# Where the activations between two matrix products begin in on-chip memory: eight starting places instead of one

## The chip, the cores and the metric

The kernel runs on one core of a Trainium2 chip. TensorE (PE) multiplies matrices: it loads a 128x128 block of weights (the stationary operand, a row "PEld LDWEIGHTS" in the trace) and then streams a second operand past it (the moving operand, "PE MATMUL"), and adds the result up in PSUM. VectorE (DVE) and ScalarE (ACT) work element by element, GpSimd (POOL) does little here, and SyncE (SP) issues most transfers from the main memory into SBUF, the on-chip memory from which both operands of a product are read. SBUF has 128 partitions; an address here is a byte offset inside a partition, the same in all 128.

The metric is the device time of one execution, in microseconds (us).

## The reference

Causal attention (2 batches, 12 heads, 448 positions, head size 64) is followed by two MLPs on the 896 rows of 768 values that it leaves. All is float32.

```python
scores = scale * np.matmul(q, k.transpose(0, 1, 3, 2))
scores = np.where(mask, -1000000000.0, scores)
attn = softmax(scores)                      # written out in the reference
x = np.matmul(attn, v) -> (896, 768)
h = np.maximum(x @ w_in, 0.0);   x = h * h @ w_out         # first MLP, 768 -> 2048 -> 768
h = x @ w_in2;  g = h - np.tanh(h);  out = g @ w_out2      # second MLP
```

## The kernel before, in words

**Attention.** For 12 pairs of heads the kernel makes scores, the exponentials, transposes of the probabilities and the product with the values. The scores, exponentials and transposes of neighbouring pairs are interleaved. The result is x, with features on the partitions: six tiles x0 to x5, each with a high and a low part (rounded value and remainder) for both batches.

**The MLPs.** Each MLP is cut in two halves of 1024 hidden features. For each half come 16 groups of the first product (8 blocks of 128 hidden features, two batches; function `first`) and then 12 groups of the second product (6 blocks of 128 output features, two batches; function `second`). A group adds up in one PSUM bank, over the blocks k of the contraction (6 in a first product, 8 in a second one), three matmuls each: high weights by high activations (line 428), high weights by low activations (line 429), low weights by high activations (line 430). Each loads 128 weights columns and streams 448 columns (one batch). So there are 4 x 16 x 6 x 3 = 1152 matmuls in the first products (PSUM tile h, moving operand x in the first MLP and y in the second) and 4 x 12 x 8 x 3 = 1152 in the second products (PSUM tile o, moving operand g).

**Between the products.** The hidden activations go through ACT and DVE (`act1`: relu and square; `act2`: the value less its tanh) and are written as a high part (line 438, ACT) and a low part (line 441, DVE) into tiles called g. One tile g holds two feature blocks of one batch, high and low: 4 x 448 words of 4 bytes. There are eight of them, in eight slots of SBUF that the attention used for its probabilities and values. Function `gdst` makes the tile when the first of its two blocks comes.

**Weights.** A weight arrives as a float64 in pieces of 128 x 768 (tile raw). DVE and ACT turn each piece into high and low float32 parts (tile w, a ring of eight). This work is woven into the rest by a budget of costs; it depends on the order of the calls alone, not on addresses.

**Addresses.** Each slot of a g tile has 64 words (256 bytes, `LINE`) more than the tile needs, so that the data can begin anywhere in the first 256 bytes. The table `G_AT` says where, by slot. Four slots begin at 192 above a multiple of 256 bytes, and four at 96; with 56 or 16 words added, every g tile begins at 160 above a multiple of 256. Inside a tile all parts lie at multiples of 256 bytes from its beginning. The tiles x and y, which SBUF's allocation puts there without a table, also begin at 160 above a multiple of 256, and all weight blocks begin at 96. So modulo 256 each moving operand of the MLPs begins 64 bytes above the weight block that it meets.

The order of all instructions and the waits between them follow from the order of the calls in the program; the change reaches the kernel through `gdst`, called by `early` (which does six groups of the first product during attention) and by `first`.

Of the kernel before, what the change touches and what calls it, by code (L numbers as in the profile page):

```python
# [27 lines left out]
NPAIR = B * NP  # L28
NQ = S // D
RING = 8  # L30
LINE = 64
G_AT = (56, 56, 56, 16, 16, 16, 16, 56)
UNIT = 6
# [52 lines left out]
def body(ctx: ExitStack, tc: tile.TileContext, qT, kT, vL, w1, w2, w3, w4, out):  # L86
# [9 lines left out]
    def slot(i, shape, dt, name):  # L96
        return sb.tile(shape, dt, tag=f"slot{i}", name=name)
# [72 lines left out]
    def ring(u):  # L170
        taken.append(u)
        return sb.tile([P, 2, UC], F32R, tag="w", bufs=RING, name=f"w{u}")

    def room():
        i = len(taken) - RING
        return i < 0 or taken[i] < freed[0]
# [317 lines left out]
    gt = {}  # L494

    def gdst(l, half, m, b):

        if m % 2 == 0:
            i = (5, 6, 0, 1, 3, 2, 4, 7)[4 * b + m // 2]
            n = 2 * 2 * S  # L500
            t = slot(i, [P, n + LINE], F32R, f"g{l}_{half}_{b}_{m // 2}")
            gt[b, m // 2] = t[:, G_AT[i] : G_AT[i] + n].rearrange("p (z k s) -> p z k s", z=2, k=2)
        t = gt[b, m // 2]
        g[m, b] = (t[:, 0, m % 2], t[:, 1, m % 2])
        return g[m, b]
# [5 lines left out]
    def first(l, half, m, b):  # L511

        u = (2 * l + half) * 2 * HALF + m
        dst = gdst(l, half, m, b)
        h = hbank(f"h{u}_{b}")
        for _ in first_pieces(l, half, m, b, h):
            pass
        if b == 1:
            freed[0] = u + 1
        return lambda: (act1, act2)[l](h, dst)  # L520


    def early(count):
        for m in range(count):
            dst = gdst(0, 0, m, 0)
            h = ps.tile([P, 512], F32, tag="h", bufs=1, name=f"h{m}_0")[:, :S]
            for k, _ in enumerate(first_pieces(0, 0, m, 0, h)):
                if k == KD - 1:
                    done.append((h, dst))
                yield  # L530
# [61 lines left out]
    for s in range(NPAIR + 2):  # L592
        p, a = s - 1, s - 2
# [162 lines left out]
```

## Time and profile before

| what | value |
|---|---|
| median of 3 runs | 541.25 us (541.24 to 541.47) |
| the profiled execution | 540.64 us |
| its span, first to last instruction | 538.9 us |
| busy PE, PEld, DVE, ACT | 532.3, 482.3, 345.9, 327.4 us |

The profiled execution has 1.7 us outside its span. "Busy" of PE counts from a matmul's start to its modelled end, and neighbouring matmuls overlap, so the distance between starts says more than the busy share: it is what the next matmul costs. The MLPs without the six early groups take the span from about 96 us to its end; attention comes before.

### The profile page before, as it was taken

The numbers are of one execution on the slowest core, as the hardware profiler recorded it, in microseconds if no ns is written. First come the engines' busy times: TensorE is split into PE (matmuls) and PEld (weight loads), VectorE is DVE, ScalarE is ACT, GpSimd is POOL, SyncE is SP. The second block draws the span as 40 slices with busy tenths as digits, with TensorE's granted clock in tenths as the row PEclk, the third lists the DMA queues.
The fourth block names the chain that finished last, engine by engine and source line by source line (L and its number), as shares of the span: only waits on it lengthen the run. The fifth ranks groups of instructions, "written<-read, shape, count | busy, mean of one in ns | idle before, by whom it ended". The sixth has DMA issues, their size and how long they took to land.

```text
span 538.9 us, 8256 instructions
## 1 busy us (share of the span) xinstructions
PE 532.3 (99%) x3206; PEld 482.3 (90%) x3206; DVE 345.9 (64%) x730; ACT 327.4 (61%) x630; POOL 3.0 (1%) x21
## 2 busy tenths in 40 slices
PE   8999999999999999999999999999999999999997
PEld 5677878899999999999999999999999999999996
DVE  6998996664525155544554688988653588887301
ACT  6999996677424276664342388876643687854100
POOL 1000000000000000000000000000000000000000
PEclk9999999999999999999999999999999999999999
DMA  8851332352534233331333230113655301026111
GB/s 312 296 191 56 115 92 98 108 185 108 182 114 140 94 121 114 117 118 58 118 111 123 65 112 0 60 58 117 234 177 177 117 1 58 1 68 220 50 52 51
DMA packets 16022, 61.86 MB, mean 115 GB/s; under 512 B 1712, under 2 KB 7344, under 8 KB 15984
## 3 DMA queue, kind: packets, MB, share of 16 engines
q1 hardware_dynamic: 15696, 61.00, 33.6%
q8 instruction: 25, 0.41, 0.3%
q10 hardware_dynamic: 288, 0.34, 0.2%
q14 instruction: 13, 0.11, 0.1%
HBM read 58.59 MB, written 2.75 MB: 114 GB/s over the span
## 4 chain that ended last, share of the span: by engine, by line
PE 92%; DVE 6%; DMA 1%; ACT 0%; issue 0%; DVEq 0%; POOLq 0%; ACTq 0%
PE h L428 15%; PE o L429 14%; PE h L429 14%; PE o L428 14%; PE h L430 14%; PE o L430 14%; PE o L380 3%; DVE p L315 3%; PE t L368 2%; DVE p L354 2%; PE s L300 2%; DMA k<-kT 1%; DVE x L416 0%; ACT pt L375 0%; DVE w L155 0%; DVE raw L139 0%
## 5 line engine op out<-in xcount | busy, mean ns | idle before, releaser
L429 PE MATMUL o<-g,w 128*128 128x448 f32 x384 | 139.4, 363 | 0.0
L428 PE MATMUL o<-g,w 128*128 128x448 f32 x384 | 139.2, 362 | 0.0
L430 PE MATMUL o<-g,w 128*128 128x448 f32 x384 | 138.2, 360 | 0.0
L428 PEld LDWEIGHTS o<-g,w 128*128 128x128 f32 x384 | 72.1, 188 | 5.7
L430 PEld LDWEIGHTS o<-g,w 128*128 128x128 f32 x384 | 71.8, 187 | 5.0
L429 PEld LDWEIGHTS o<-g,w 128*128 128x128 f32 x384 | 72.1, 188 | 3.7
L428 PE MATMUL h<-x,w 128*128 128x448 f32 x192 | 71.4, 372 | 0.0
L429 PE MATMUL h<-x,w 128*128 128x448 f32 x192 | 69.7, 363 | 0.0
L429 PE MATMUL h<-y,w 128*128 128x448 f32 x192 | 69.7, 363 | 0.0
L428 PE MATMUL h<-y,w 128*128 128x448 f32 x192 | 69.6, 362 | 0.0
L430 PE MATMUL h<-x,w 128*128 128x448 f32 x192 | 69.3, 361 | 0.0
L430 PE MATMUL h<-y,w 128*128 128x448 f32 x192 | 69.1, 360 | 0.0
L139 DVE SCALAR_TENSOR_TENSOR raw<-raw 128x768 int32<-128x768 int32 x64 | 61.0, 954 | 11.7 <-ACT raw L125 11.7
L142 ACT CAST w<-raw 128x768 fp32r<-128x768 f32 x56 | 50.3, 898 | 26.7 <-DVE raw L139 26.7
L125 ACT ACTIVATE raw<-raw 128x768 f32<-128x768 f32 x64 | 58.7, 917 | 0.0
L155 DVE TENSOR_TENSOR w<-raw,w 128x768 fp32r<-128x768 f32 x32 | 30.6, 957 | 34.3 <-ACT w L142 34.1
L441 DVE TENSOR_TENSOR g<-r,g 128x448 fp32r<-128x448 f32 x32 | 20.0, 624 | 41.1 <-ACT g L438 41.1
L570 ACT COPY part<-o 128x448 f32<-128x448 f32 x24 | 12.8, 533 | 55.1 <-PE o L430 55.1
L153 DVE SCALAR_TENSOR_TENSOR w<-w,raw 128x768 fp32r<-128x768 f32 x32 | 30.6, 956 | 23.0 <-ACT w L142 22.9
L333 ACT ACTIVATE p<-p,st 128x320 f32<-128x320 f32 (+6 forms) x84 | 41.0, 512 | 3.3 <-DVE st L315 3.2
L428 PEld LDWEIGHTS h<-x,w 128*128 128x128 f32 x192 | 36.1, 188 | 3.1
L428 PEld LDWEIGHTS h<-y,w 128*128 128x128 f32 x192 | 36.0, 188 | 2.9
(57 smaller groups left out, 722.8 us busy)
## 6 DMA issues: line engine op xcount, KB each, us to landing
raw<-w SPq DMA_DIRECT2D x64, 768.0 KB, 4.2
q<-qT SPq DMA_DIRECT2D x12, 224.0 KB, 4.9
k<-kT SPq DMA_DIRECT2D x11, 224.0 KB, 3.8
out<-part SPq DMA_DIRECT2D x11, 224.0 KB, 1.9
v<-vL SPq DMA_DIRECT2D x2, 576.0 KB, 7.0
v<-vL SPq DMA_DIRECT2D x1, 1152.0 KB, 6.0
k<-kT ACTq DMA_DIRECT2D x1, 224.0 KB, 3.6
vend<-vL SPq DMA_DIRECT2D x2, 96.0 KB, 6.9
```

Source lines behind the costliest of these rows:

```text
L125: nc.scalar.activation(h, h, AF.Prelu, scale=2.0**-112, alpha=2.0**32)
L139: nc.vector.scalar_tensor_tensor(out=lo, in0=hi, scalar=3, in1=lo, op0=ALU.logical_shift_left, op1=ALU.bitwise_or)
L142: act_late.append(lambda: nc.scalar.copy(out=st["w"][:, 0], in_=lo.bitcast(F32)))
L153: nc.vector.scalar_tensor_tensor(out=w[:, 1], in0=w[:, 0].bitcast(F32), scalar=-(1.0 - 2.0**-24), in1=f, op0=ALU.mult, op1=ALU.add)
L155: nc.vector.tensor_sub(out=w[:, 1], in0=f, in1=w[:, 0])
L315: nc.vector.tensor_tensor_reduce(out=prob[n % 3][:, POFF[c] : POFF[c] + w], in0=sc.pop((n, c)), in1=mask[:, BEFORE - D * DIAG[c] :][:, :w] ...
L333: nc.scalar.activation(p, p, AF.Exp, bias=st[:, 0, i : i + 1], scale=-1.0, **kw)
L380: return nc.tensor.matmul(ob[n][D * j : D * j + D, o], lhsT=vs[b][kc][rows, D * h : D * h + D], rhs=rhs, skip_group_check=True, **flags).ins
L428: nc.tensor.matmul(h, lhsT=hi, rhs=xh, start=(k == 0), stop=False)
L429: nc.tensor.matmul(h, lhsT=hi, rhs=xl, start=False, stop=False)
L430: nc.tensor.matmul(h, lhsT=lo, rhs=xh, start=False, stop=(k == kk - 1))
L441: nc.vector.tensor_sub(out=dst[1], in0=v, in1=dst[0])
```

## The change

A second table, by layer, half and batch, is added to the place of the first one, modulo 64 words. Nothing else is changed: the tiles' sizes, slots, order and waits are the same, and the instruction streams of all engines are the same row by row apart from line numbers.

```diff
 RING = 8
+G_ADD = (56, 60, 62, 4, 12, 24, 28, 36)
 LINE = 64
 G_AT = (56, 56, 56, 16, 16, 16, 16, 56)
...
             t = slot(i, [P, n + LINE], F32R, f"g{l}_{half}_{b}_{m // 2}")
-            gt[b, m // 2] = t[:, G_AT[i] : G_AT[i] + n].rearrange("p (z k s) -> p z k s", z=2, k=2)
+            at = (G_AT[i] + G_ADD[4 * l + 2 * half + b]) % LINE
+            gt[b, m // 2] = t[:, at : at + n].rearrange("p (z k s) -> p z k s", z=2, k=2)
```

In bytes, modulo 256, the g tiles then begin as follows; the last column is the distance from the weight blocks (at 96), which is 64 in all eight cases before. Each row stands for 144 matmuls.

| layer, half, batch | g begins at | above the weights by |
|---|---|---|
| first MLP, half 0, batch 0 | 128 | 32 |
| first MLP, half 0, batch 1 | 144 | 48 |
| first MLP, half 1, batch 0 | 152 | 56 |
| first MLP, half 1, batch 1 | 176 | 80 |
| second MLP, half 0, batch 0 | 208 | 112 |
| second MLP, half 0, batch 1 | 0 | 160 |
| second MLP, half 1, batch 0 | 16 | 176 |
| second MLP, half 1, batch 1 | 48 | 208 |

The tiles x and y, and with them all first products, stay at a distance of 64.

## Rows read from the trace of the kernel before

**Rows 1.** Page: the span, and parts 1 and 2 (PE and granted clock)

```profile
span 538.9 us, 8256 instructions
...
PE 532.3 (99%) x3206; PEld 482.3 (90%) x3206; DVE 345.9 (64%) x730; ACT 327.4 (61%) x630; POOL 3.0 (1%) x21
...
PE   8999999999999999999999999999999999999997
...
PEclk9999999999999999999999999999999999999999
```

**Rows 2.** Page, part 4: the chain that ended last, by engine

```profile
PE 92%; DVE 6%; DMA 1%; ACT 0%; issue 0%; DVEq 0%; POOLq 0%; ACTq 0%
```

**Rows 3.** Stretches: length, busy us (count) of PE, PEld, DVE, ACT; second: tile g

```profile
109.68:533.88 424.20, 424.20 (x2123) 397.60 (x2122) 251.60 (x380) 233.56 (x373) 0.00 (x0) 1.00 0.31 104
...
96.00:540.00 444.00, 231.05 (x1152) 215.95 (x1152) 36.66 (x59) 32.48 (x58) 1.00 0.31 103
```

**Rows 4.** Order of time: start us, us, engine, line; first products, then second, then the end

```profile
109.67 0.36 PE L428 MATMUL h<-x,w 128*128 128x448 f32 x1
...
110.27 0.36 PE L428 MATMUL h<-x,w 128*128 128x448 f32 x1
...
299.87 0.36 PE L428 MATMUL o<-g,w 128*128 128x448 f32 x1
299.87 0.19 PEld L429 LDWEIGHTS o<-g,w 128*128 128x128 f32 x1
...
300.07 0.36 PE L429 MATMUL o<-g,w 128*128 128x448 f32 x1
...
300.47 0.36 PE L428 MATMUL o<-g,w 128*128 128x448 f32 x1
...
533.87 0.36 PE L428 MATMUL o<-g,w 128*128 128x448 f32 x1
```

**Rows 5.** Groups by form: count, busy us, mean ns of one, idle us before

```profile
L428 PEld LDWEIGHTS o<-g,w 128*128 128x128 f32 x384 | 72.1, 188 | 5.7
...
L430 PEld LDWEIGHTS o<-g,w 128*128 128x128 f32 x384 | 71.8, 187 | 5.0
...
L429 PEld LDWEIGHTS h<-y,w 128*128 128x128 f32 x192 | 36.0, 188 | 1.8
...
L368 PEld LDWEIGHTS t<-ident,p 128*128 128x128 f32 x168 | 19.0, 141 | 4.6 <-issue 1.3 <-DVE p L354 1.0 <-ACT pt L375 0.5
```

**Rows 6.** Groups that write g and wait, 98 to 536 us, same columns; then two waits

```profile
L441 DVE TENSOR_TENSOR g<-w,g 128x448 fp32r<-128x448 f32 x32 | 19.8, 618 | 4.5 <-ACT g L438 4.5
...
L438 ACT CAST g<-w 128x448 fp32r<-128x448 f32 x32 | 17.7, 554 | 3.1 <-DVE w L480 3.1
...
L441 DVE TENSOR_TENSOR g<-r,g 128x448 fp32r<-128x448 f32 x27 | 16.9, 625 | 40.7 <-ACT g L438 40.7
...
L438 ACT CAST g<-r 128x448 fp32r<-128x448 f32 x26 | 14.8, 568 | 0.8
...
ACT part L570 <- PE o L430: 55.1, 22, 4.3
...
ACT r L445 <- PE h L430: 23.1, 24, 3.0
```

## The prediction, on record before the changed kernel ran

> **What bounds the kernel now.** I read the page first. PE is busy 532.3 of 538.9 us, and the granted clock is full in all 40 slices [rows 1], which is the 2.4 GHz level. The chain that ended last is 92% PE [rows 2]. So, after attention, the time is the number of matmuls by the distance between their starts, and nothing else counts unless it makes PE wait.
>
> The windows give that distance. From 109.68 to 533.88 us PE is busy for all of the 424.20 us, with 2123 matmuls [rows 3]. Two of them began before the window, so 2121 starts share 424.20 us: 200.0 ns each. The order of time shows it at both ends: L428 starts at 109.67 and 110.27 in a first product, at 299.87 and 300.47 in a second one, and the stretch ends with a start at 533.87, so three matmuls take 0.60 us, and 707 such steps of 0.60 us are exactly the 424.20 us [rows 4]. There is not one gap, and x, y and g cost the same, whatever slot the g tile is in and whatever weight block it meets. Addresses that differ by multiples of 256 bytes therefore make no difference here; what no row of this kernel varies is the distance modulo 256, which is 64 everywhere.
>
> The groups show what the 200.0 ns hold. At 2.4 GHz and one column a tick, 448 columns need 186.7 ns; the rest is an excess of 13.3 ns. The next weight load starts together with a matmul (299.87 and 299.87 [rows 4]) and takes 187 to 188 ns, in second and first products alike, while a load of the same 128 columns takes 141 ns beside the short matmuls of the transposes [rows 5]. So beside a stream of 448 columns a load is 188 - 141 = 47 ns longer, and it ends some 12 ns before the next matmul starts. I read it thus: PE's two reads, of weights and of moving data, hold each other up, and the load ends late enough that it may be what spaces the matmuls. The trace can't prove the second half of that.
>
> **The change part by part.** It adds, removes and reorders no instruction, wait or transfer. It has three edits in effect.
>
> First, writes. ACT writes the high part and DVE the low part of g in new places. From 98 us on these are 26 + 32 writes of 568 and 554 ns on ACT, and 27 + 32 of 625 and 618 ns on DVE [rows 6], 69.2 us together. I price the edit at nothing: in the long stretch ACT is busy 233.56 and DVE 251.60 of 424.20 us [rows 3], and ACT waits 55.1 us for PE before L570 and 23.1 us before L445 [rows 6]. Were each write 10% longer, 6.9 us more would go into 363 us of idle time. Only the last writes ahead of a second product have little time; 10% of a pair of 554 and 618 ns is 0.12 us, so with four products that bounds the loss at 0.5 us. A gain there can't reach PE, since PE waits for nothing.
>
> Second, the first products. x and y stay where they are: 1152 matmuls, no change.
>
> Third, the second products: 1152 matmuls with the moving operand g, together 231.05 us of PE's busy time [rows 3]. Their distance from the weights goes from 64 bytes to 32, 48, 56, 80, 112, 160, 176 and 208, 144 matmuls each. Each ns by which the mean distance between starts changes is 1152 x 1 ns = 1.15 us. No row shows another distance, so I bound it. Below: the whole excess goes, 13.3 x 1152 = 15.4 us less; a stream can't be shorter than its columns. Above there is no such floor: the excess may double, 15.4 us more, and if the load took its 47 ns once more and every matmul waited for it, 54.1 us more. That last end is far from any row, since all 707 steps show the reads mostly hidden; I keep the doubling as the upper bound that counts.
>
> Which value? The slack on the two sides is unequal. A load that ends earlier can give back no more than 13.3 ns; a load that ends later pushes the next matmul at once, with 12 ns between them. Where two streams meet is set by their phase, so I expect places near the old one (32, 48, 56 and 80, all within 32 bytes of 64, the first MLP) to cost about what it costs, and those far from it (112, 160, 176 and 208, the second MLP) to lie between no change and a doubling. I take half the excess for these, 6.7 ns, midway because no row is nearer to either end: 144 x 4 x 6.7 ns = 3.85 us, and nothing for the near four. The profiled execution, 540.64 us, becomes 544.5; the median of the runs lies 0.6 us above that execution, so 545.1 us.
>
> The Trainium skill speaks against a change: its page "TensorE: Matmul & The Clock Gate", section "Step-by-step: what each phase is for", says that weights and moving data come through two independent read ports, so that loading the next weights takes no bandwidth from the running matmul; the page "SBUF — State Buffer", section "Who interferes with whom", adds that PE waits for no one. By that rule the time would be 541.25 us. The 188 ns load beside 141 ns [rows 5] does not fit it without more; it is the rule behind the first rival.
>
> **The rivals.** No effect of the address. Then all second products keep 200.0 ns, and the time is 541.25 us, within 0.2% (1.1 us, about what a measurement of this kernel can tell from no change). For it: no engine's work disturbs the 0.60 us steps, x, y and g agree to the row, and the 141 ns of the transposes may owe to their shorter stream, so that the 188 ns is merely how a load beside a long stream is recorded. Against: the excess of 13.3 ns is there, and the one quantity that could move it is never varied. The same time comes out if near and far places balance. 0.17.
>
> Faster: 64 bytes is a bad distance, and the loads meet the stream most there. Moving off it lets a load end sooner, until the stream bounds alone. If half the places lose the whole excess, 576 x 13.3 ns = 7.7 us go: 533.6 us; if a quarter of it goes everywhere, 3.8 us: 537.4 us. It decides from a mean of 199.1 ns on. For it: the excess exists, so there is something to win. Against: three matmuls take 600 ns in every step, with nothing that looks like a worst case, and the floor is close. 0.16.
>
> Slower by more: the near four suffer as the far four do, or the excess doubles in most places. All eight at a full doubling give 541.25 + 15.4 = 556.6 us; beyond that the load would bound openly. It is the upper part of my own case: 0.19 of its 0.67 above 550 us. A mechanism for it is the start of the stream: if the first reads of weights and data fall on the same piece of memory, the load falls behind at once and does not catch up.
>
> That the change does not do what it says: the starting places follow from the slots' addresses, and none of the eight is 64 above the weights, so this has no chance of its own. A second bound can't take PE's place: DVE has 172.6 us idle in the stretch [rows 3].
>
> **How the numbers follow.** Slower by places far from 64: 0.67, with 545.1 us and its own range of 542.4 to 556.6. No effect: 0.17, 541.25. Faster: 0.16, 537.4 for most of it, 526 at the floor. I count 0.66 slower, 0.18 same and 0.16 faster, since a little of the first case is too small to see. The range goes from 539.0 (the faster case's smaller half inside) to 556.6 (the doubling): some 0.10 is left out below and 0.08 above.
>
> **What would show it.** The order of time gives each second product by itself. Right: first products still at 0.60 us for three matmuls; in the second MLP's second products three matmuls take about 0.62 us (200.0 + 6.7 ns each), in the first MLP's 0.60 us; the granted clock stays 1.00; weight loads of the slower groups take longer than 188 ns; the steps alternate between the two batches of one half, since these have different places. Wrong in size: all eight moved, or only one place (152, the only one that is no multiple of 16). Wrong in kind: 0.60 us everywhere, or less than 0.60 us in any second product; or unchanged steps and a PE that idles before second products, which would mean the writes of g.

## The result, and the profile after

The changed kernel takes 545.09 us (median of 3 runs, 544.98 to 545.39) against 541.25 us: the ratio is 1.0071, with a 95% interval of 1.0048 to 1.0094. It is slower by 3.84 us, as forecast in sign and size (545.1 us). The parts of the forecast were less good than their sum, as the rows and runs below show.

The profiled execution has a span of 543.2 us, 4.3 us more than before. The page of the kernel after answers to [rows 1, 2]:

```profile
span 543.2 us, 8256 instructions
...
PE 536.4 (99%) x3206; PEld 482.7 (89%) x3206; DVE 346.2 (64%) x730; ACT 327.7 (60%) x630; POOL 3.0 (1%) x21
...
PEclk9999999999999999999999999999999999999999
...
PE 92%; DVE 6%; DMA 1%; issue 0%; ACT 0%; DVEq 0%; POOLq 0%; ACTq 0%
```

PE's busy time grew by 4.1 us; DVE and ACT have what they had, and the clock is full. Next, the long stretch [rows 3] cut at the borders of the products: from the first second product to the last, in turn second (g), first (x or y), second and so on. The columns are the stretch, its length, and busy us with counts for PE, PEld, DVE, ACT and POOL, then the clock, the DMA share and GB/s.

```profile
131.79:190.71 58.92, 58.92 (x290) 54.10 (x289) 21.51 (x28) 20.68 (x30) 0.00 (x0) 1.00 0.37 121
190.71:248.31 57.60, 57.60 (x290) 53.98 (x288) 28.84 (x40) 40.43 (x64) 0.00 (x0) 1.00 0.36 123
248.31:306.82 58.51, 58.51 (x290) 54.05 (x288) 29.81 (x44) 20.16 (x28) 0.00 (x0) 1.00 0.28 95
306.82:364.42 57.60, 57.60 (x289) 53.99 (x288) 51.42 (x87) 46.67 (x83) 0.00 (x0) 1.00 0.16 55
364.42:423.01 58.59, 58.59 (x290) 53.98 (x289) 33.99 (x46) 29.23 (x41) 0.00 (x0) 1.00 0.48 162
423.01:480.61 57.60, 57.60 (x290) 53.99 (x288) 49.01 (x83) 46.69 (x83) 0.00 (x0) 1.00 0.17 55
480.61:539.20 58.59, 58.59 (x288) 54.02 (x287) 24.49 (x36) 12.79 (x17) 0.00 (x0) 1.00 0.24 84
```

Each product has 288 matmuls. First products keep 288 x 200.0 ns = 57.60 us, to some 0.01 us. Second products take 58.92, 58.51 and 58.59 us, and the fourth takes 58.60 us from 480.61 to its last start at 539.21, 287 steps, for which 287 x 200.0 ns = 57.40 us would do: 1.32 + 0.91 + 0.99 + 1.2 = 4.4 us more. The first of them began 0.1 us earlier than before (131.78 against 131.87 us), which leaves the 4.3 us of the span. PE is busy for the whole of each stretch, so no wait was added.

Inside one second product the two batches alternate in groups of 24 matmuls. The order of time of the kernel after (start us, duration us, engine, line) has these first matmuls of groups, one pair of groups from the first second product and one from the third:

```profile
151.42 0.37 PE L429 MATMUL o<-g,w 128*128 128x448 f32 x1
...
156.37 0.36 PE L429 MATMUL o<-g,w 128*128 128x448 f32 x1
...
161.24 0.37 PE L429 MATMUL o<-g,w 128*128 128x448 f32 x1
...
383.96 0.36 PE L429 MATMUL o<-g,w 128*128 128x448 f32 x1
...
388.90 0.37 PE L429 MATMUL o<-g,w 128*128 128x448 f32 x1
...
393.72 0.36 PE L429 MATMUL o<-g,w 128*128 128x448 f32 x1
```

In the first MLP's half 0, batch 0 (distance 32) takes 4.95 us for 24, or 206 ns each, and batch 1 (48) 4.87 us, or 203 ns. In the second MLP's half 0, batch 0 (112) takes 4.94 us and batch 1 (160) 4.82 us, or 201 ns. From the starts of all matmuls, three of them take on average, by distance (600 everywhere before):

| distance | 32 | 48 | 56 | 80 | 112 | 160 | 176 | 208 |
|---|---|---|---|---|---|---|---|---|
| ns for three | 618.5 | 609.0 | 609.5 | 609.4 | 617.8 | 602.6 | 612.9 | 612.1 |

Each stands for 48 triples: 48 x (18.5 + 9.0 + 9.5 + 9.4) = 2.2 us in the first MLP and 48 x (17.8 + 2.6 + 12.9 + 12.1) = 2.2 us in the second.

Weight loads in the kernel after, by form (count, busy us, mean ns, idle us), answer to [rows 5]:

```profile
L430 PEld LDWEIGHTS o<-g,w 128*128 128x128 f32 x384 | 72.1, 188 | 6.2
L431 PEld LDWEIGHTS o<-g,w 128*128 128x128 f32 x384 | 72.1, 188 | 6.1
```

They still take 188 ns, although the matmuls behind them start later: the first sign that the end of the load is not what spaces the matmuls.

### The profile page after: what moved, and what is told of

Its sections match the earlier page's. It is cut to its first block, busy times and chain, and to the rows that moved or that the text cites. A ratio compares the mean times of both kernels' runs of the same rounds, so it can differ in the third digit from the quotient of the medians.

```text
span 543.2 us, 8256 instructions
## 1 busy us (share of the span) xinstructions
PE 536.4 (99%) x3206; PEld 482.7 (89%) x3206; DVE 346.2 (64%) x730; ACT 327.7 (60%) x630; POOL 3.0 (1%) x21
## 3 DMA queue, kind: packets, MB, share of 16 engines
HBM read 58.59 MB, written 2.75 MB: 113 GB/s over the span
## 4 chain that ended last, share of the span: by engine, by line
PE 92%; DVE 6%; DMA 1%; issue 0%; ACT 0%; DVEq 0%; POOLq 0%; ACTq 0%
PE o L430 14%; PE o L431 14%; PE o L429 14%; PE h L429 14%; PE h L430 14%; PE h L431 14%; PE o L381 3%; DVE p L316 3%; PE t L369 2%; DVE p L355 2%; PE s L301 2%; DMA k<-kT 1%; DVE x L417 0%; ACT pt L376 0%; DVE raw L140 0%
## 5 line engine op out<-in xcount | busy, mean ns | idle before, releaser
L430 PE MATMUL o<-g,w 128*128 128x448 f32 x384 | 140.5, 366 | 0.0
L431 PE MATMUL o<-g,w 128*128 128x448 f32 x384 | 140.5, 366 | 0.0
L429 PE MATMUL o<-g,w 128*128 128x448 f32 x384 | 140.5, 366 | 0.0
```

Source lines behind the costliest of these rows:

```text
L429: nc.tensor.matmul(h, lhsT=hi, rhs=xh, start=(k == 0), stop=False)
L430: nc.tensor.matmul(h, lhsT=hi, rhs=xl, start=False, stop=False)
L431: nc.tensor.matmul(h, lhsT=lo, rhs=xh, start=False, stop=(k == kk - 1))
```

## The experiments

Theory D: the cost of a matmul follows the distance, modulo 256 bytes, at which its stream begins from the weights that are loaded beside it. Rivals: the stream's own place (A), the stage of the program (S), and a hidden better distance (F). The times of before that ran beside these kernels lie at 540.9 us; from there the change costs 4.2 us, which is nearer to the 4.3 us of the two spans.

**All operands 32 bytes further, distances kept.**

```diff
+    pad = sb.tile([P, 8], F32, name="pad")
+    nc.vector.memset(pad, 0.0)
     ident = sb.tile([P, P], F32, name="ident")
```

> Theory D (what counts is the distance between the moving data and the weights, modulo 256 bytes): every operand stands 32 bytes further, all distances stay 64, so three matmuls still take 0.600 us in all products and the time is 541.2 us (540.5 to 542). Rival A (what counts is the place of the moving data itself, modulo 256): x, y and g all begin at 192 instead of 160; with places as costly as those of the changed kernel (603 to 619 ns for three) all 2304 matmuls would cost 1 to 6 ns more, 543 to 555 us.

Measured: 540.96 against 540.95 us, ratio 1.0002 (0.9992 to 1.0012). The windows give 57.60 us for second and first products. Place alone (A) is out, at least for a shift of 32 bytes.

**The eight places in reverse order.**

```diff
-G_ADD = (56, 60, 62, 4, 12, 24, 28, 36)
+G_ADD = (36, 28, 24, 12, 4, 62, 60, 56)
```

> The eight places of the changed kernel in the reverse order of layer, half and batch. Theory D: the cost goes with the place, so first MLP half 0 batch 0 (now 208) takes about 612 ns for three matmuls instead of 618, second MLP half 1 batch 1 (now 32) about 618 instead of 612, second MLP half 0 batch 0 (now 80) 609, first MLP half 1 batch 0 (now 160) 603; the time stays at 545 us. Rival S (it goes with the stage: what ACT and DVE do beside, or the data): the old order of costs stays with the stages, 618 in the first MLP's half 0 batch 0 and 603 in the second MLP's half 0 batch 1.

Measured: 545.39 us (one run). Three matmuls take 612.0, 612.8, 602.5, 617.4, 609.4, 609.5, 608.9 and 618.6 ns in the order of layer, half and batch: the costs moved with the places, within 0.4 ns. The stage (S) is out. The same two places still take turns within each half, so this does not tell what a place costs without its neighbour.

**Half of the change, near and far.** First the four near places alone, then the four far ones.

```diff
-G_ADD = (56, 60, 62, 4, 12, 24, 28, 36)
+G_ADD = (56, 60, 62, 4, 0, 0, 0, 0)     # first MLP alone; the other kernel: (0, 0, 0, 0, 12, 24, 28, 36)
```

> Only the first MLP's four places of the change (32, 48, 56, 80); the second MLP's g at 64 as before. Theory D with the costs read from the changed kernel's trace (18.5, 9.0, 9.5 and 9.4 ns for three matmuls, 48 times each): 2.2 us more than the kernel before, 543.2 us. Rival, as the prediction had it (places within 32 bytes of 64 cost nothing): 541.0 us.

> Only the second MLP's four places (112, 160, 176, 208). Theory D from the same trace (17.8, 2.6, 12.9, 12.1 ns): 2.2 us more, 543.2 us, with the groups at 160 free to come out higher, since all eight at 160 showed two patterns. Rival, as the prediction had it (all of the cost is here): 3.85 us more, 544.8 us.

Measured: 543.13 us (ratio 1.0040, 1.0028 to 1.0053) and 543.17 us (1.0040, 1.0026 to 1.0054), each 2.2 us above 540.93. The halves add up, and the near one costs as much as the far one. In the near-only kernel the first second product takes 58.92 us and the third 57.60:

```profile
132.31:191.23 58.92, 58.92 (x289) 54.10 (x288) 21.49 (x28) 20.75 (x30) 0.00 (x0) 1.00 0.36 121
...
364.95:422.55 57.60, 57.60 (x289) 53.99 (x288) 33.98 (x46) 29.03 (x41) 0.00 (x0) 1.00 0.50 165
```

**Eight other distances.**

```diff
-G_ADD = (56, 60, 62, 4, 12, 24, 28, 36)
+G_ADD = (48, 52, 0, 8, 16, 20, 32, 44)  # 0, 16, 64, 96, 128, 144, 192, 240 bytes
```

> Eight other distances: 0, 16, 64, 96, 128, 144, 192, 240 in the order of layer, half, batch. Theory D: the 144 matmuls at 64 (first MLP, half 1, batch 0) take 600 ns for three as before; the others lie between 600 and 620, the time between 541 and 548 us. Rival F (64 is no floor; some distance gets nearer to the 560 ns that three streams of 448 columns need at 2.4 GHz): at least one place below 597 ns.

Measured: 545.47 us (one run); 620.2, 606.5, 600.8, 615.5, 612.2, 619.4, 607.0 and 608.1 ns in that order. Only 64 is near 600, and its 0.8 comes from the groups' first matmuls, behind those at 96. F finds nothing here.

**All eight at 72, at 40 and at 160 bytes.**

```diff
-G_ADD = (56, 60, 62, 4, 12, 24, 28, 36)
+G_ADD = (2,) * 8          # 72 bytes; the others: (58,) * 8 for 40, (24,) * 8 for 160
```

> All eight g places at a distance of 72 bytes, only 8 bytes from 64, where the matmuls alone settled at 208.3 ns. Theory D: 625 ns for three in all second products, 1152 x 8.3 ns = 9.6 us more, 550.5 us. Rival N (cost grows with the distance from 64, so a near place costs little): under 604 ns for three, 542 us or less.

> All eight g places at a distance of 40 bytes from the weights, where the matmuls alone settled at 200.0 ns. Theory D (distance modulo 256 alone): three matmuls of the second products take 600 ns but for a few behind each change from another distance, and the time is that of the kernel before, 541 us (540.7 to 541.8). Rival A64 (64 bytes is the only good place in the kernel, since what stands around differs from the matmuls alone): 609 ns or more for three as at 32, 48 and 56, 544 us or more.

> All eight g places at a distance of 160 bytes. In the changed kernel the groups at 160 ran at 200 ns from their sixth matmul on, and cost more only in the first five behind each group at 112. Theory D with patterns that carry over: with one place for all, the first five are paid once in each second product, three matmuls take 600 ns, and the time is that of the kernel before within 0.2% (540 to 542 us). Rival (160 has its own cost, or slips out of the pattern within a group as 40 did): 603 ns or more, 542.5 us or more.

Measured at 72: 548.74 us (1.0147, 1.0132 to 1.0162), 620 ns for three and not 625. Eight bytes from 64 the price is 7.9 us, so nearness to 64 (N) protects nothing. At 40: 543.59 us (1.0051, 1.0034 to 1.0068), neither of the two expectations: two of every eight triples take 621 to 622 ns and the others 600 to 603, 606.6 on average. At 160 my expectation failed: most runs are at 548.2 to 548.9 us, two of ten at 540.7 and 541.4 us. The profiled one has 620 ns for three throughout:

```profile
131.87:191.38 59.51, 59.51 (x289) 53.89 (x288) 21.42 (x28) 20.75 (x30) 0.00 (x0) 1.00 0.35 120
191.38:248.99 57.61, 57.61 (x290) 54.02 (x289) 28.82 (x40) 40.55 (x64) 0.00 (x0) 1.00 0.37 123
```

So one program with one set of addresses has two rhythms. The profiled execution stays at 207 ns in all four second products; neither of the two short ones was profiled, and that they ran at some 200 ns is read from their times: four second products of 59.51 instead of 57.60 us are 7.6 us, about the difference between the two kinds of run. Beside 112, in the changed kernel, the same 160 costs 602.6 ns, so what a place costs can depend on its neighbour.

**The low part alone moved, to 112.**

```diff
-            t = slot(i, [P, n + LINE], F32R, f"g{l}_{half}_{b}_{m // 2}")
-            gt[b, m // 2] = t[:, G_AT[i] : G_AT[i] + n].rearrange("p (z k s) -> p z k s", z=2, k=2)
+            t = slot(i, [P, n + 2 * LINE], F32R, f"g{l}_{half}_{b}_{m // 2}")
+            gt[b, m // 2] = [t[:, at : at + n // 2].rearrange("p (k s) -> p k s", k=2) for at in (G_AT[i], G_AT[i] + n // 2 + 12)]
         t = gt[b, m // 2]
-        g[m, b] = (t[:, 0, m % 2], t[:, 1, m % 2])
+        g[m, b] = (t[0][:, m % 2], t[1][:, m % 2])
```

> The high part of g at a distance of 64 as before, the low part 48 bytes further, at 112 (207 ns alone). Theory D read by the single matmul: the matmul that streams the low part (line 429) costs 207 and the two others 200, 606 ns for three, 1152 / 3 x 6.7 = 2.6 us more, 543.5 us. Rival P (the pattern of the reads goes on from one matmul to the next, so that a change of distance inside a group unsettles all three): each of the three costs more, or any value from 600 to 620 comes out, 541 to 549 us.

Measured: 546.15 us (one run), 613.3 ns for three: 201.7 for line 428, 209.2 for line 429, which streams the low part, and 202.5 for line 430. Of the 13.3 ns the moved stream pays 9.2, and the two that stayed at 64 pay 2.5 and 1.7. Theory D read by the single matmul (207, 200 and 200 ns) holds for the larger part, its rival P, by which all three pay, for the rest.

**Matmuls alone.** A kernel of runs of matmuls with fixed operands, by distance (d) and kind; s moves weights and stream together. The means are from the sixth matmul of a run on.

```python
for n in range(LOADS):
    at = (s // size) + P * (n % 6)
    a = (d + s) % 256 // size
    lhsT = (w if kind == "f" else wb)[:, at : at + cols]
    nc.tensor.matmul(o, lhsT=lhsT, rhs=t[:, a : a + S], start=(n == 0), stop=(n == LOADS - 1))
```

> No attention and no MLP, only runs of 30 matmuls by kind: 32 distances from 0 to 248 bytes, then loads of 64 weight columns at five distances, then weights and moving data shifted together, then bf16. The output is not the reference's. Theory D with the load as what spaces the matmuls: distance 64 gives 200 ns between starts, 32 and 112 about 207, 160 settles at 200; with 64 columns to load the load is done early and all five distances fall to about 187 to 190 ns; shifted together the cost stays; bf16, which reads half the bytes, shows no distance. Rival W (the stream waits at the weight reads, each costing it a fixed time, and the end of the load does not matter): 64 columns give about half of the excess, some 193 ns, and still differ by distance.

Measured: of 32 distances in steps of 8 bytes none settles below 200.0 ns; 16, 40, 64 and 168 settle there, 72 and 248 highest at 208.3. At 160 it was 206.7 here, not 200. With 64 weight columns the loads end after 133 to 138 ns, yet the matmuls still take 200.3, 201.7, 205.0, 201.6 and 202.2 ns at 32, 64, 112, 160 and 208: both of my expectations for this fell (187 to 190 ns everywhere, or some 193). With 128 columns these five distances take 206.7, 200.0, 206.7, 206.7 and 204.0 ns, so shorter loads make four of them cheaper and 64 dearer, and none comes below 200. bf16 takes 189.2 ns at all three distances.

A second kernel of that kind varied the columns and the shifts:

> Runs of 40 matmuls alone, the output is not the reference's. By kind: 128, 64, 32 and 8 weight columns; 256, 320, 384 and 512 moving columns; a series of distances and shifts one after the other; bf16; bf16 with every second element streamed. Distances 64, 112 and 72. Theory R (the excess over the stream comes from reads of 4-byte weights meeting those of the 4-byte stream): with 8 weight columns it is near bf16's 2.5 ns at all distances, and with 128 it is 13 to 22 ns whatever the number of moving columns. Rival M (the 4-byte stream costs it by itself): about 13 ns with 8 weight columns too, or an excess that grows with the moving columns; bf16 over every second element then costs more than 189 ns. In the series, theory D has the same cost each time a distance returns; rival H (what came before decides between several patterns): 160 settles at 200 once and 207 the other time, and a shift of both by 16 bytes differs from none.

Its order of time has one row for each run of 40 (start us, length us): names ca to cd are 128, 64, 32 and 8 weight columns, with x, y, z for distances 64, 112 and 72; nax and nay stream 256 columns; sa, sb and sc are distance 64 with both operands moved by 0, 16 and 0 bytes; ba, bb and bc are bf16 at 64, 112 and 72, va, vb and vc the same over every second element.

```profile
23.93 8.16 PE L85 MATMUL o<-cax,w 128*128 128x448 f32 x40
31.93 8.43 PE L85 MATMUL o<-cay,w 128*128 128x448 f32 x40
40.20 8.49 PE L85 MATMUL o<-caz,w 128*128 128x448 f32 x40
48.53 8.21 PE L85 MATMUL o<-cbx,w 128*64 128x448 f32 x40
...
64.77 8.16 PE L85 MATMUL o<-cbz,w 128*64 128x448 f32 x40
72.77 8.42 PE L85 MATMUL o<-ccx,w 128*32 128x448 f32 x40
...
97.17 8.40 PE L85 MATMUL o<-cdx,w 128*8 128x448 f32 x40
105.41 8.30 PE L85 MATMUL o<-cdy,w 128*8 128x448 f32 x40
113.54 8.33 PE L85 MATMUL o<-cdz,w 128*8 128x448 f32 x40
121.70 4.87 PE L85 MATMUL o<-nax,w 128*128 128x256 f32 x40
126.41 4.75 PE L85 MATMUL o<-nay,w 128*128 128x256 f32 x40
...
202.04 8.17 PE L85 MATMUL o<-sa,w 128*128 128x448 f32 x40
210.05 8.41 PE L85 MATMUL o<-sb,w 128*128 128x448 f32 x40
218.29 8.16 PE L85 MATMUL o<-sc,w 128*128 128x448 f32 x40
...
299.38 7.75 PE L85 MATMUL o<-ba,wb 128*128 128x448 bf16 x40
306.97 7.73 PE L85 MATMUL o<-bb,wb 128*128 128x448 bf16 x40
314.53 7.73 PE L85 MATMUL o<-bc,wb 128*128 128x448 bf16 x40
322.10 8.03 PE L85 MATMUL o<-va,wb 128*128 128x448 bf16 x40
329.97 8.07 PE L85 MATMUL o<-vb,wb 128*128 128x448 bf16 x40
337.88 8.16 PE L85 MATMUL o<-vc,wb 128*128 128x448 bf16 x40
```

From start to start: 8.00 us for ca at 64 (200 ns each), but 8.24 us for 8 weight columns at the same distance (206 ns). At 72 it is the other way round: 8.33 us with 128 weight columns and 8.00 us with 64. In ns between starts, from the sixth matmul of a run on, by the number of weight columns:

| distance | 128 | 64 | 32 | 8 |
|---|---|---|---|---|
| 64 | 200.0 | 201.6 | 206.7 | 206.7 |
| 112 | 206.7 | 205.2 | 203.5 | 203.4 |
| 72 | 208.4 | 200.0 | 200.0 | 203.9 |

The loads, by form:

```profile
L85 PEld LDWEIGHTS o<-cax,w 128*128 128x128 f32 x40 | 7.5, 188 | 0.5
...
L85 PEld LDWEIGHTS o<-nax,w 128*128 128x128 f32 x40 | 4.8, 188 | 0.1
...
L85 PEld LDWEIGHTS o<-cdx,w 128*8 128x8 f32 x40 | 3.5, 88 | 4.7
```

At distance 64 a load of 88 ns ends some 116 ns before the next start, and the matmul is no cheaper. With 256 columns streamed the matmuls start 117.8 ns apart (4.71 us from nax to nay), although each load is still recorded at 188 ns, so the loads overlap one another. So the end of the load is not what sets the distance between starts, and 188 ns is not the mark of a long stream: my reading of [rows 4, 5] is refuted. So is theory R in its forecast that 8 weight columns come near bf16's cost at all distances. But the load does take part: the number of weight columns changes the cost by up to 8.4 ns, up at 64 and down at 72 and 112. What no number of them changes is that nothing settles below 200.0 ns.

bf16 costs 189 ns (7.56 us from bb to the next run), but the same bf16 over every second element, which passes over as many bytes as the 4-byte stream, 196.7, 197.8 and 200.0 ns at 64, 112 and 72. M, by which the 4-byte stream costs it by itself, holds in part: of what the 4-byte operands cost above bf16 (10.8, 17.5 and 19.2 ns) the bytes that the stream passes over bring 7.5, 8.6 and 10.8. At distance 64 the excess is no fixed share of the columns: 256 columns take 117.8 ns (106.7 at full rate), 384 take 173.3 (160.0), 512 take 228.9 (213.3). At 72 it grows with them, from 11.6 ns with 256 columns to 22.3 with 512. And at distance 64 a shift of both by 16 bytes turns 200 ns into 206.7 (sb), each time it was tried, one of 48 bytes does the same, and those of 32 and 64 bytes do not; distance alone is not all of it.

The last kernel repeats this in the kernel's own sequence of weights (high, high, low) and streams (high, low, high).

```python
kk, z = divmod(n, 3)
at = s // 4 + P * (kk % 6)
a = (d + s) % 256 // 4 + S * (kk % 2) + 2 * S * (z == 1)
nc.tensor.matmul(o, lhsT=w[:, int(z == 2), at : at + P], rhs=t[:, a : a + S], start=(n == 0), stop=(n == LOADS - 1))
```

> Matmuls alone in the kernel's own sequence (high weights twice, low weights once; high, low, high part of the moving data; two blocks in turn), 30 for each case: all distances in steps of 4 bytes, then weights and moving data both 16 and both 8 bytes further in steps of 8, then a series that comes to 160 from 152, 64, 152 and 112. The output is not the reference's. Theory D: no case settles below 199.5 ns, so that no place can beat the kernel before; 64, 160 and some others at 200, most between 202 and 209; 40 at 202 as in the kernel and not 200 as with one block alone. Rival F: a case settles at 198 ns or less; applied to all 2304 matmuls that would be 4.6 us or more below the kernel before. In the series: if what came before decides, 160 settles at 200 behind 64 and 112 and at 207 behind 152; if the place alone decides, at one value all four times.

Measured: all cases settle between 200.0 and 211.0 ns (mean from the sixth matmul on). Of the distances without a shift only 64 and 160 settle at 200.0. With weights and stream both 8 bytes further it is 40, 56, 136 and 184 that settle there, and 64 takes 206.5; with both 16 bytes further 64 takes 206.6. So the place of the weights counts as well as the distance. Distances 40 (pba), 64 (pbg), 72 (pbi) and 160 (pea), 30 matmuls each:

```profile
84.29 6.23 PE L85 MATMUL o<-pba,w 128*128 128x448 f32 x30
90.35 6.21 PE L85 MATMUL o<-pbb,w 128*128 128x448 f32 x30
...
120.78 6.17 PE L85 MATMUL o<-pbg,w 128*128 128x448 f32 x30
126.80 6.36 PE L85 MATMUL o<-pbh,w 128*128 128x448 f32 x30
133.00 6.35 PE L85 MATMUL o<-pbi,w 128*128 128x448 f32 x30
139.19 6.18 PE L85 MATMUL o<-pbj,w 128*128 128x448 f32 x30
...
268.37 6.17 PE L85 MATMUL o<-pea,w 128*128 128x448 f32 x30
274.37 6.39 PE L85 MATMUL o<-peb,w 128*128 128x448 f32 x30
```

That is 6.06, 6.02, 6.19 and 6.00 us: 202, 201, 206 and 200 ns with the first few of each run. 40 has the 202 it has in the kernel. In the closing series 160 came out at 200.0 all four times, behind 152, 64 and 112 alike. The second kernel of matmuls alone had it at 200.0 twice, the first one at 206.7; what stood just before it does not explain that, since behind 152 it was 206.7 in the one and 200.0 here. F is out for all places tried, so no version beat the kernel before, and none was built.

## Why the prediction was right, point by point

**The bound.** Right. PE fills every stretch, 407.41 us of the rows' 407.41 from 131.79 us on, and the whole loss lies in the distance between starts.

**Writes of g.** Right at nothing: first products, beside which most of these writes run, keep 57.60 us, and no wait of PE appears.

**First products.** Right, to some 0.01 us.

**Second products.** The sum came out and its terms did not. I had nothing for the near four places and 144 x 4 x 6.7 ns = 3.85 us for the far four; the trace gives 2.2 and 2.2 us, and the two kernels with half of the change give 2.2 us each. The step that failed is "I expect places near the old one (...) to cost about what it costs": the near four cost 3.9 ns a matmul, and at 72, 8 bytes off, the price is among the highest. The far four cost 3.8 ns a matmul, not 6.7. I had the near four 2.2 us too low and the far four 1.7 us too high, and the 0.6 us by which I let the median lie above the profiled execution was 0.1 us this time (545.09 and 544.98). That these errors cancel to within 0.1 us is luck.

**The reason.** That the place of the stream against the weights decides was right (all shifted together by 32 bytes, places reversed), though common shifts of 8 and 16 bytes show that the distance is not the whole of it. That PE's two reads affect each other fits, since the number of weight columns changes the cost, but where they do so no run shows. That the end of the load spaces the matmuls was wrong: I took the 12 ns between load and next start [rows 4, 5] for a chain, and a load that ends 116 ns ahead does not bring the matmul below 200.0 ns. The argument that losses have more room than gains led to the right sign and is borne out otherwise: 64 sits on the lowest value that any case with 448 columns of 4 bytes reached, 200.0 ns, so moving off it could only lose or draw. The excess of 13.3 ns, which I let the faster rival win back, was not won by any distance tried.

**The independent ports.** The Trainium skill's "TensorE: Matmul & The Clock Gate", section "Step-by-step: what each phase is for", has weights and stream read through independent ports, without cost to the matmul. For bf16 the runs agree: 189.2 ns at all distances tried. The same page of the Trainium skill, section "Wait — 56ns, not 53.3ns?", gives columns at the clock and some 2.5 ns, for 448 columns an estimate of 186.7 + 2.5 = 189.2 ns, as measured. For 4-byte operands the runs do not agree: 200.0 to 211.0 ns by distance alone, and 200.0 to 208.4 ns at 72 bytes by the number of weight columns.

**What would show it.** First products, the alternation of the batches and the clock came as said. The 0.60 us of the first MLP and the 0.62 us of the second did not: three matmuls take 609 to 619 ns in the one and 603 to 618 ns in the other. All eight places moved, which I had named as the sign of a forecast that is wrong in size. Longer loads did not come (188 ns still), nor did a special price for the place at 56 (152 modulo 256), the only one that is no multiple of 16: 609.5 ns, like its neighbours.

**Open.** Where in the stream the two reads meet, why fewer weight columns cost more at 64 and less at 72 and 112, why common shifts of 8, 16 and 48 bytes matter at 64 and those of 32 and 64 do not, and what chooses between the two rhythms at 160.

## What to carry to other kernels

Where PE is the bound and streams 4-byte data, look at the time between matmul starts, not at the busy time, and compare it with the columns at the granted clock; if an excess is left, the starting places of weights and stream, modulo 256 bytes, are worth a sweep with matmuls alone, in the kernel's own sequence. Nearness to a good place is no safety, and a place should be kept only if it holds from any start: 64 did in every kernel here in which loads had 128 columns and the weights began at a multiple of 32 bytes, 160 did not.

## What the runs showed of the hardware that was not expected

- 4-byte matmuls of 448 columns settle into steady rhythms that depend on the distance of the stream from the weights and on the place of the weights: 200.0 ns at best, 206.7 ns at many distances, up to 211.0; bf16 takes 189.2 ns at each of the four distances tried.
- With all g at 160 bytes one program took 541 us in two executions and 548 us in eight, which fits two rhythms of some 200 and 207 ns.
- The number of weight columns moves the cost either way: with 128, 64, 32 and 8 of them matmuls at distance 64 settle at 200.0, 201.6, 206.7 and 206.7 ns, at 72 at 208.4, 200.0, 200.0 and 203.9.
- A load of 128 columns is recorded at 188 ns even where matmuls of 256 columns start 118 ns apart; its recorded length is no bound on their distance.
